# Attention's q-times-kv product in quarter tiles of the tensor engine

## The chip, the cores and the metric

The kernel runs on one core of a Trainium2 chip. The metric is the device time of one execution in microseconds; a number for a kernel is the median of several executions. Below, PE is the tensor engine, PEld its weight loads (which overlap PE: on the page before, PEld is busy for 95% of the span and PE for 100%), DVE, ACT and POOL are the vector, scalar and GpSimd engines, and SP issues most transfers. L649 is line 649 of the kernel. The change adds two lines, so L651 afterwards is L649 before, L868 is L866, and so on.

## The reference, cut to what matters

```python
batch, n_heads, seq, head_dim = (8, 8, 576, 64)
kv  = np.einsum('bhsd,bhse->bhde', k, v)
out = np.einsum('bhsd,bhde->bhse', q, kv)          # the product that the change touches
rms = np.sqrt(np.mean(out * out, axis=-1, keepdims=True) + 1e-06)
x   = out / rms * g_norm                           # then reshaped to (4608, 512)
for e in range(4):                                 # four experts, 512 -> 1024 -> 512
    h = np.maximum(x @ w1[e], 0.0)
    y += p[:, e:e + 1] * (h @ w2[e])           # p: the given weights of the experts, summing to 1
```

Everything is f32. The four experts are nearly all of the work; attention is done batch by batch during the first expert.

## The kernel before

A small planner in the kernel lays out every operation in advance on every engine: each has a key (its place), a cost, and the buffers that it reads and writes. Tensor instructions then stand in the program in that fixed order. Where the planner expects the tensor engine to wait at the start, it puts fillers, products whose result nobody uses, so that the engine is busy there too (in the profile before, its granted clock was 1.00 from 4.30 us to 1748.51):

```python
    def idle(bank):                       # one filler: 2 transposes of the identity
        for r in range(2):
            nc.tensor.transpose(bank[:, r * P:(r + 1) * P], ident[:], ident[:])
```

The part in question, for one batch and one group of four heads (two pairs `o`; heads of a pair lie in the upper and the lower 64 rows; `P` = 128, `D` = 64, `NR` = 4 tiles of 128 tokens):

```python
            raw = [Buf("ab" if b > 1 else "db", f"raw{b}_{g}_{r}") for r in range(2)]

            def attend(eng, raw=raw, g=g):
                for o in range(2):
                    for i in range(NR):
                        for r in range(2):
                            half = slice(r * D, (r + 1) * D)
                            nc.tensor.matmul(
                                raw[r].ap[:, (o * NR + i) * D:(o * NR + i + 1) * D],
                                lhsT=qTs[2 * g + o].ap[half, i * P:(i + 1) * P],
                                rhs=kv[g].ap[half, o * D:(o + 1) * D],
                            )

            plan.add(at(2 * g + 1.4), {"PE": 1.0}, attend, ...)
            # ... then ACT squares the result, DVE sums and scales it, PE transposes it
```

q is the stationary operand: 64 rows (one head) by 128 tokens. Two row halves, each with its own PSUM bank, take part. There are 8 x 2 = 16 such blocks of 16 matmuls. The 64 tokens left over in each batch have a like product of their own (L710).

## Time and profile before

| | before |
|---|---|
| time, median of 3 runs | 1753.49 us (1751.84 to 1754.53) |
| span of the profiled execution | 1750.2 us |
| PE busy, share of the chain that ended last | 100%, 99% |
| next busiest engine | DVE, 66% |
| the 16 blocks of L649 | 16 x 1.93 us = 31 us |

The point in reading it is to take durations of tensor records for what they are. A matmul of L649 "lasts" 272 ns, but one pair of them starts every 111.7 ns. Here only the times of starts give the rate. The lines that show this stand in the prediction.

### The profile page before, as it was taken

Reading aid. Unit: us, or ns where it says so; the run is one execution under the profiler, and the core shown is the slowest. Engines: PE = TensorE matmul, PEld = TensorE weight load, DVE = VectorE, ACT = ScalarE, POOL = GpSimd, SP = SyncE. Lnnn points to the kernel's source line nnn. Section 1 sums busy time; section 2 is a strip of 40 time slices with the busy share of each in tenths; the row PEclk is TensorE's granted clock in tenths of the full one; section 3 lists DMA queues with packets and bytes.
Section 4 is the critical chain, followed back from the end, with each engine's and each line's share of the span. In section 5 each row is a group of like instructions: output and inputs, shape, how many; then the busy total and the mean of one; then the engine's idle time right before and its main releaser. Section 6 shows DMA issues by size and latency. Waiting matters only on the chain.

```text
span 1750.2 us, 36758 instructions
## 1 busy us (share of the span) xinstructions
PE 1741.5 (100%) x14568; PEld 1663.4 (95%) x14568; DVE 1154.8 (66%) x1745; ACT 917.7 (52%) x2234; POOL 702.0 (40%) x684
## 2 busy tenths in 40 slices
PE   9999999999999999999999999999999999999998
PEld 7799999999999999999999999999999999999998
DVE  2765554555665467777786567777787567777774
ACT  2454544454444456666555456666655446666662
POOL 2633332332333524333356624333345724333331
PEclk9999999999999999999999999999999999999999
DMA  9755534541443334444456434444456434444442
GB/s 222 231 176 173 167 114 133 164 139 61 176 134 116 107 97 109 109 109 109 121 157 156 99 97 109 109 109 110 109 157 169 104 92 109 113 110 108 110 104 49
DMA packets 148588, 220.83 MB, mean 126 GB/s; under 512 B 49600, under 2 KB 90816, under 8 KB 148416
## 3 DMA queue, kind: packets, MB, share of 16 engines
q1 hardware_dynamic: 133312, 191.21, 34.7%
q0 software_dynamic: 15104, 27.27, 11.2%
q8 instruction: 114, 1.87, 0.4%
q14 instruction: 58, 0.48, 0.1%
HBM read 145.30 MB, written 73.14 MB: 125 GB/s over the span
## 4 chain that ended last, share of the span: by engine, by line
PE 99%; DMA 0%; DVE 0%; SPq 0%; ACT 0%; issue 0%
PE u L866 44%; PE db L1080 17%; PE db L1155 16%; PE ab L1155 10%; PE ab L1080 4%; PE u L953 2%; PE ab L629 2%; PE ab L649 1%; PE ab L616 1%; PE ab L1289 1%; PE ab L668 1%; PE db L649 0%; PE ab L710 0%; DMA small<-in_q_dram 0%; PE db L668 0%; PE ab L693 0%
## 5 line engine op out<-in xcount | busy, mean ns | idle before, releaser
L866 PE MATMUL u<-xf,big 128*128 128x128 f32 x3536 | 509.3, 275 | 0.0
L360 DVE TENSOR_TENSOR big<-big,big 128x1024 f32<-128x1024 f32 (+1 forms) x420 | 464.2, 1117 | 56.1 <-ACT big L849 26.0
L866 PEld LDWEIGHTS u<-xf,big 128*128 128x128 f32 x3536 | 456.1, 192 | 4.3
L866 PE MATMUL u<-xf,w1y 128*128 128x128 f32 x2652 | 383.0, 276 | 0.0
L893 DVE TENSOR_TENSOR big<-u,snap 128x256 f32<-128x256 f32 x446 | 188.2, 422 | 260.1 <-PE u L866 195.4
L866 PEld LDWEIGHTS u<-xf,w1y 128*128 128x128 f32 x2652 | 342.1, 192 | 3.8
L885 ACT ACTIVATE snap<-u 128x256 f32<-128x256 f32 x490 | 187.9, 383 | 241.2 <-PE u L866 202.7
L1080 PE MATMUL db<-big,big 128*128 128x256 f32 x1192 | 280.4, 380 | 0.0
L1080 PEld LDWEIGHTS db<-big,big 128*128 128x128 f32 x1192 | 216.3, 190 | 24.5
L360 POOL TENSOR_TENSOR big<-big,big 128x256 f32<-128x256 f32 (+1 forms) x125 | 161.1, 1303 | 162.3 <-DVE big L360 64.8
L885 ACT ACTIVATE big<-u 128x256 f32<-128x256 f32 x446 | 170.4, 383 | 106.0 <-PE u L866 77.3
L360 POOL TENSOR_TENSOR big<-big 128x512 f32<-128x512 f32 (+1 forms) x75 | 91.1, 1215 | 161.5 <-DVE big L360 120.7
L849 ACT ACTIVATE big<-big 128x1024 f32<-128x1024 f32 x124 | 130.1, 1051 | 7.6 <-DVE big L360 4.8
L1155 PE MATMUL db<-big,big 128*128 128x128 f32 x788 | 113.0, 275 | 0.0
L1221 POOL TENSOR_TENSOR big<-big 128x512 f32<-128x512 f32 x19 | 24.2, 1271 | 217.8 <-DVE big L360 164.1
L1183 ACT ACTIVATE snap<-db 128x256 f32<-128x256 f32 (+1 forms) x168 | 60.0, 357 | 94.4 <-PE db L1155 88.0
L885 ACT ACTIVATE u<-u 128x256 f32<-128x256 f32 x245 | 91.0, 371 | 29.0 <-PE u L866 12.4
L1155 PEld LDWEIGHTS db<-big,big 128*128 128x128 f32 x788 | 100.3, 192 | 0.0
L1027 ACT ACTIVATE big<-db,p_all 128x256 f32<-128x256 f32 x90 | 42.6, 474 | 109.1 <-PE db L1080 109.1
L1050 POOL DMA_DIRECT2D out_dram<-big x98 | 88.6, 991 | 21.9 <-ACT big L1027 16.3
L1155 PE MATMUL db<-kv,big 128*128 128x128 f32 x624 | 88.6, 275 | 0.0
L1155 PE MATMUL ab<-kv,big 128*128 128x128 f32 x588 | 84.1, 275 | 0.0
(208 smaller groups left out, 2650.4 us busy)
## 6 DMA issues: line engine op xcount, KB each, us to landing
xf<-x SPq DMA_DIRECT2D x108, 512.0 KB, 3.6
out_dram<-big POOLq DMA_DIRECT2D x82, 256.0 KB, 5.5
xf<-x_h SPq DMA_DIRECT2D x81, 256.0 KB, 3.1
xf<-x SPq DMA_DIRECT2D x81, 256.0 KB, 3.3
x<-xf SPq DMA_DIRECT2D x36, 512.0 KB, 3.1
big<-in_moe_w_dram SPq DMA_DIRECT2D x28, 512.0 KB, 5.2
small<-in_q_dram SPq DMA_DIRECT2D x72, 128.0 KB, 4.1
kv<-in_k_dram SPq DMA_DIRECT2D x30, 288.0 KB, 3.7
```

The source lines that it names most:

```text
L360: lambda eng: adder(eng).tensor_tensor(out=out_(), in0=a(), in1=b(), op=op),
L629: nc.tensor.matmul(bank.ap[r * D:(r + 1) * D, o * D:(o + 1) * D], lhsT=kv_rows(kt)[:, r, j, :], rhs=kv_rows(vt)[:, r, j, :], start=(j == 0 ...
L849: lambda eng: nc.scalar.activation(out=b.ap[:], in_=b.ap[:], func=ACT.Relu),
L866: nc.tensor.matmul(ps.ap[:, u * P:(u + 1) * P], lhsT=w1f[e][m][mm][1]()[:, u * P:(u + 1) * P], rhs=views[m][mm][1](), start=(mm in (1, 5) ...
L885: lambda eng: nc.scalar.activation(out=where(), in_=ps.ap[:, 0:HN], func=ACT.Copy),
L893: lambda eng: nc.vector.tensor_tensor(out=block(whole, a, t), in0=src.ap[:, 0:HN], in1=add_.ap[:], op=ALU.add),
L953: nc.tensor.matmul(bank.ap[:], lhsT=two(w.ap[:])[:, kt, ut * P:(ut + 1) * P], rhs=two(xh[dh].ap[:])[:, kt, :], start=(dh == kt == 0), stop ...
L1027: lambda eng: nc.scalar.activation(out=cell(i, half), in_=ap(), func=ACT.Copy, scale=prob()),
L1050: nc.gpsimd.dma_start(out=dst, in_=cell(i)[parts, :], accum_op=ALU.add)
L1080: nc.tensor.matmul(ps.ap[:, 0:HN], lhsT=four(h[m])[:, kt // 2, t, kt % 2, :], rhs=w2f[e][m].ap[:, kt * HN:(kt + 1) * HN], start=(m in (1, ...
L1155: nc.tensor.matmul(ps.ap[:, o * P:(o + 1) * P], lhsT=b.ap[:, col:col + P], rhs=w2q[e][m][mm][1]()[:, kt, :], start=(mm in (1, 5) and o == ...
L1183: lambda eng: nc.scalar.activation(out=where(), in_=group_of(ps.ap), func=ACT.Copy),
```

## The change

The 128 tokens of a tile are cut into two column halves of 64, so that a matmul uses 64 rows by 64 columns, one quarter of the 128*128 of the trace's full-array products. Four such quarters hold two heads by two halves of tokens. The intent is that 64 columns of weights make a step about half as long as 128 do (58.3 ns in L710 and 111.7 in L649, in the trace before), and that all four quarters work together. The results land in the same places of PSUM.

```diff
-                        for r in range(2):
-                            half = slice(r * D, (r + 1) * D)
-                            nc.tensor.matmul(
-                                raw[r].ap[:, (o * NR + i) * D:(o * NR + i + 1) * D],
-                                lhsT=qTs[2 * g + o].ap[half, i * P:(i + 1) * P],
-                                rhs=kv[g].ap[half, o * D:(o + 1) * D],
-                            )
+                        for c in range(2):
+                            for r in range(2):
+                                half = slice(r * D, (r + 1) * D)
+                                at = i * P + c * D
+                                nc.tensor.matmul(
+                                    raw[r].ap[c * D:(c + 1) * D, (o * NR + i) * D:(o * NR + i + 1) * D],
+                                    lhsT=qTs[2 * g + o].ap[half, at:at + D],
+                                    rhs=kv[g].ap[half, o * D:(o + 1) * D],
+                                )
```

## The prediction

> **What bounds the kernel now.** I read the page first, because its shares say which engine can matter at all.
>
> ```profile
> PE 1741.5 (100%) x14568; PEld 1663.4 (95%) x14568; DVE 1154.8 (66%) x1745; ACT 917.7 (52%) x2234; POOL 702.0 (40%) x684
> ...
> PEclk9999999999999999999999999999999999999999
> ...
> PE 99%; DMA 0%; DVE 0%; SPq 0%; ACT 0%; issue 0%
> ```
>
> The tensor engine is busy through the whole span of 1750.2 us, its clock is granted in every slice, and the chain of work that ended last is tensor work for 99%. The next engine, DVE, is at 66%. A microsecond taken from the tensor engine's stream should therefore be a microsecond of the end, unless something else was waiting just behind. The list of waits shows how little the tensor engine waited:
>
> ```profile
> PE ab L616 <- DMA small<-in_q_dram: 1.9, 1, 1.9
> PE ab L1289 <- POOL ident masks.py:199: 1.4, 1, 1.4
> PE ab L1289 <- ACT small L621: 0.7, 1, 0.7
> ```
>
> All three lie in the first 21 us. After that nothing makes it wait.
>
> Next, the groups by shape, for the line that is changed, L649 (q times the key-value block), and for two relatives that already use parts of the new form:
>
> ```profile
> L629 PE MATMUL ab<-kv,kv 96*64 96x64 f32 x720 | 27.3, 226 | 0.0
> ...
> L649 PE MATMUL ab<-kvbd,small 64*128 64x64 f32 x384 | 24.0, 275 | 0.0
> ...
> L649 PE MATMUL db<-kvbd,small 64*128 64x64 f32 x128 | 8.0, 275 | 0.0
> ...
> L710 PE MATMUL ab<-kvbd,small 64*64 64x64 f32 x112 | 4.8, 224 | 0.0
> ```
>
> Here 64*128 is active rows by columns of weights. L649 has 384 + 128 = 512 records: 8 batches x 2 groups x 16 matmuls x 2, because each f32 matmul stands in the trace as two weight loads and two passes. So the whole changed line costs 32 us, 1.8% of the span. That is the ceiling for anything done to it, and already says that a gain over 2% cannot come. The mean of 275 ns is a latency, not a rate; the rate has to come from starts. One block in the timeline:
>
> ```profile
> 79.87 0.61 PE L866 MATMUL u<-big,w1y 128*128 128x128 f32 x4
> ...
> 80.41 1.86 PEld L649 LDWEIGHTS ab<-kvbd,small 64*128 64x128 f32 x32
> 80.41 2.00 PE L649 MATMUL ab<-kvbd,small 64*128 64x64 f32 x32
> ...
> 82.34 0.44 PE L668 MATMUL db<-ident,big 128*128 128x128 f32 x2
> ```
>
> The block keeps the engine from 80.41 to 82.34, 1.93 us. All 16 such blocks take 1.93 us to the next line's first matmul, save one with 1.84. The single records inside it start in pairs, 6.7 ns apart; the first pair is followed by the second 160 ns later, the others every 111.7 ns, 16 pairs in all. A pair is the upper and the lower row half: they run together, and the pair's step is the time to load 128 columns of weights, the same 111.7 ns as one full-array record of L866.
>
> The remainder's attention (L710) uses the same row halves, but with 64 columns of weights:
>
> ```profile
> 114.41 0.68 PE L710 MATMUL ab<-kvbd,small 64*64 64x64 f32 x16
> 115.02 0.38 PE L866 MATMUL u<-small,big 128*128 128x128 f32 x1
> ```
>
> Its records also start in pairs 6.7 ns apart, with the second pair 107 ns after the first and then a pair every 58.3 ns; 148 ns after its last start the next line starts. The key-value products (L629) are two column halves of 64 on the same rows, and there too a pair starts every 58.3 ns. So row halves overlap, column halves overlap, and 64 columns make the step 58.3 ns. What the trace has nowhere is both splits at once.
>
> [...] a change of shape costs 203 to 206 ns between starts, where 111.7 would do. [...] a full-array matmul has its wait on the first of its two records and its signal on the second, but a block of L649 has its waits, where it has any, on records 0 and 1 and its two signals, one for each row half's bank, on records 30 and 31 of 0 to 31. So first pass, first pass, second pass, second pass: the halves are interleaved.
>
> **The change part by part.** I compared the two programs' instruction orders. DVE, ACT, POOL and SP have the same instructions in the same order; on the tensor engine 256 matmuls (128 columns of weights) become 512 (64 columns) in the same places. The planner's cost for the block was left at 1.0, so nothing moves. Both programs' waits are at the same places. There is no other work to pay for: results land in the same PSUM partitions.
>
> One block, if four tiles run together: 32 matmuls x 2 passes = 64 records = 16 rounds of four. Taking L710's steps: 107 ns to the second round, 14 x 58.3 = 816 for the others, 3 x 6.7 = 20 within the last round: 943 ns from first to last start. Then 148 ns to the next line, as L710 has it: 1091 ns. The issue itself fits: four load-and-multiply couples x 6.7 = 27 ns, under 58. Before: 1932. Saved: 0.84 us a block, and 16 x 0.84 = 13.5 us.
>
> What of it reaches the end? From 70 us on, all of it, I think. In the stretches of 60 us between 138 and 378, DVE is busy for 31 to 33 us and ACT for 29, so a stream that is 1.7 us shorter in each finds them idle enough. At the front inputs arrive just in time. The block at 15.14 comes before L629 at 21.97, whose v landed at 21.25: 0.72 slack against 0.84 earlier, so some 0.1 is lost. The block at 26.90 comes before the L953 at 28.83, whose last quarter of w1 landed at 27.13: 1.70 of slack against 0.72 + 0.84 = 1.56, nothing lost. I put 0.3 for the front in all. 13.5 - 0.3 = 13.2; 1753.5 - 13.2 = 1740.3 us.
>
> **The rivals.** First, only two tiles at a time. The four tiles are issued as four matmuls of two passes each; to have four in flight the engine must reach past the second passes of three tiles, where today it reaches past one. That it does so for one is what the waits and signals above show. If two is the limit, a block is 32 pairs: 107 + 30 x 58.3 + 7 + 148 = 2011 ns, 0.08 more than before, x 16 = +1.3 us: 1754.8. For it speaks that every split in the trace shows pairs and never more; against it, that no line now offers more than two tiles, and that even pairs kept in order would do: the second passes of one pair can run beside the first passes of the next pair, which uses the other two tiles. Chance 0.13.
>
> Second, the supply of instructions. A block becomes 128 instructions (64 loads, 64 passes) in 0.94 us. [...] Against it: the tensor engine shows 95% weight-load occupancy with no such stall; but its usual couple takes 111.7 ns, so this proves little. Chance of a noticeable loss 0.17.
>
> Third, tiles that don't overlap at all in the 64x64 mode: 64 x 58.3 + 148 = 3.88 us a block, +31 us: 1784.6. L629 and L710 speak against it. 0.02.
>
> Fourth, the gain is there, but an engine behind eats it: ACT squares the results and the transposes wait for DVE and POOL. The block at 104.36 has its transposes at 122, that at 137.26 at 148.5, 10 us and more later, so I give it only the 0.3 us above.
>
> **Range and chances.** The first way has about 0.65 and gives 1740.3, with 1.5 us either side for runs that differ (before: 1751.84 to 1754.53). The other cases pull the point up a little: 1741.0. An 80% range must hold the case of two tiles as well: 1737.5 to 1755.0. Over 2% faster would need 35 us, more than the line costs: 0.01. Over 2% slower needs more than the serial case: 0.02. Within 2%: 0.97.
>
> **What will show it.** L649's successor (L651) has 1024 matmul records with 64*64. Right: starts in fours every 58 ns, block 1.09 us, the line's busy time near 18 us (it counts about 0.1 of tail a block), the tensor engine's waits no longer than before save some tenths at 20 to 30 us. Two-tile limit: pairs every 58 ns, block 2.0 us. Supply:[...] wider gaps with "issue" named as their cause. Eaten gain: new waits on ACT or DVE before the transposes (L670), or on DMA in the first 70 us. Wrong altogether: a block longer than 2.1 us, or changed intervals in other lines.

## The result, and the profile after

The changed kernel took 1741.53 us (median of 4 runs, 1738.37 to 1743.82) against 1752.66 (1751.42 to 1754.53) for the kernel before, runs of both being in the fast state. The ratio is 0.9934, interval 0.9915 to 0.9953. A ratio here is the mean time of one kernel's fast runs over that of the other's of the same rounds, so it is not quite the ratio of the medians; a gain in microseconds below is (1 - ratio) x the mean of the kernel before. Here that is 0.0066 x 1752.8 = 11.6 us.

The page's engine line and chain, after:

```profile
PE 1730.4 (99%) x15080; PEld 1651.8 (95%) x15080; DVE 1151.7 (66%) x1745; ACT 918.0 (53%) x2234; POOL 701.8 (40%) x684
...
PE 99%; DMA 0%; SPq 0%; DVE 0%; issue 0%; POOL 0%; ACT 0%; POOLq 0%
```

There are 512 more tensor records (15080 - 14568), yet PE is busy for less, and it is still 99% of the chain. The groups by shape, with the changed line now 64 rows by 64 columns and twice as many records:

```profile
L651 PE MATMUL ab<-kvbd,small 64*64 64x64 f32 x768 | 13.9, 221 | 0.0
...
L651 PE MATMUL db<-kvbd,small 64*64 64x64 f32 x256 | 4.6, 221 | 0.0
```

The line's busy time fell from 32.0 to 18.5 us. The timeline around the same block as in the prediction (start, length, engine, line):

```profile
80.17 0.61 PE L868 MATMUL u<-big,w1y 128*128 128x128 f32 x4
...
80.71 1.16 PE L651 MATMUL ab<-kvbd,small 64*64 64x64 f32 x64
...
81.80 0.66 PE L670 MATMUL db<-ident,big 128*128 128x128 f32 x4
```

The block keeps the engine from 80.71 to 81.80, 1.09 us, and so do all 16 blocks (1.091 to 1.093). Single records start in fours, 6 to 7 ns apart; the second four comes 107 ns after the first, then one every 58.3 ns. The two signals of a block, one for each bank, stand on records 62 and 63 of 0 to 63 (7 of the 16 blocks have a third signal, on 61). Four quarters do work together, and the saving is 0.84 us a block, 13.4 us in all.

But look at the first of these times. The block started at 80.41 before and starts at 80.71 now, although four blocks lie in front of it. By then 4 x 0.84 = 3.36 us should have been gained; 0.30 have been lost. So the front of this execution gave back 3.7 us. From there on nothing is lost: the block at 399.05 before starts at 390.11 after, so that the stretch of eleven blocks from the fifth to the sixteenth is 9.24 us shorter, 11 x 0.84, and the spans differ by 1750.2 - 1740.4 = 9.8 us, which is 13.4 less some 3.6. The list of waits of the tensor engine after the change:

```profile
PE ab L1291 <- issue: 2.1, 1, 2.1
PE ab L1291 <- POOL ident masks.py:199: 1.4, 1, 1.4
PE ab L616 <- DMA small<-in_q_dram: 1.0, 2, 0.5
PE ab L1291 <- ACT small L621: 0.7, 1, 0.7
PE ab L629 <- DMA kv<-in_v_dram: 0.2, 1, 0.2
```

There is a wait of 2.1 us that was not there, and "issue" says that the profile sees no semaphore and no transfer of data to blame. The timeline shows where it is:

```profile
17.38 0.92 PE L629 MATMUL ab<-big,big 96*64 96x64 f32 x24
20.38 0.60 PE L1291 MATMUL ab<-ident 128*128 128x128 f32 x4 [2.08 <-issue]
20.81 0.60 PE L616 MATMUL ab<-ident,small 128*128 128x128 f32 x4
22.10 1.89 PE L1291 MATMUL ab<-ident 128*128 128x128 f32 x8 [0.69 <-ACT small L621]
23.92 1.55 PE L629 MATMUL ab<-big,big 96*64 96x64 f32 x24
```

The same stretch in the kernel before, without a stop:

```profile
18.32 0.92 PE L629 MATMUL ab<-big,big 96*64 96x64 f32 x24
19.17 0.66 PE L1289 MATMUL ab<-ident 128*128 128x128 f32 x4
...
20.95 1.09 PE L1289 MATMUL ab<-ident 128*128 128x128 f32 x8 [0.69 <-ACT small L621]
21.97 0.92 PE L629 MATMUL ab<-big,big 96*64 96x64 f32 x24
```

The changed kernel's engine stops before a filler (L1291), which reads nothing but the identity. And after the stop it is slow: eight filler records take 1.89 us where the kernel before took 1.09, and 24 records of L629 take 1.55 in place of 0.92. The busy times by stretch, with the granted clock of PE third from the end, show why (columns: stretch, its length, then busy time and records of PE, PEld, DVE, ACT, POOL, clock, DMA share, GB/s):

```profile
18.30:20.40 2.10, 0.02 (x2) 0.09 (x2) 0.32 (x1) 0.00 (x0) 1.60 (x2) 1.00 1.04 315
22.22:25.64 3.42, 3.42 (x33) 2.97 (x34) 1.04 (x2) 0.12 (x1) 0.00 (x0) 0.50 1.13 332
```

After the stop the clock was halved for 3.41 us, which costs half of that, 1.7. Together with the 2.1 us of the stop this is 3.8, and about the loss. What halves the clock this trace doesn't show; in as long a stretch up to the halving (18.81 to 22.22) the engine was busy for 1.16 us.

What was the engine waiting for? The trace has transfers of the kind "instruction". Queue 8 has 114 of them, packets of 16,384 bytes, before and 118 after; 2 x 14568 tensor records / 114 is 256 records a packet, and the 4 more packets go with 1024 more records. So the tensor engine's own instructions arrive in blocks of 256. I numbered the tensor engine's instructions (loads, passes, semaphores and one drain at the head) by their starts. The stop comes directly after the 449th. The first instruction packet was in flight from 17.62 to 18.86 us, and the 450th instruction starts at 20.38. In the kernel before the same packet landed at 19.29, and the 449th instruction was not due until 22.43. That the stop is a wait for this packet is my inference from these times.

### The profile page after: what moved, and what is told of

Its sections match the earlier page's. It is cut to its first block, busy times and chain, and to the rows that moved or that the text cites. A ratio compares the mean times of both kernels' runs of the same rounds, so it can differ in the third digit from the quotient of the medians.

```text
span 1740.4 us, 37793 instructions
## 1 busy us (share of the span) xinstructions
PE 1730.4 (99%) x15080; PEld 1651.8 (95%) x15080; DVE 1151.7 (66%) x1745; ACT 918.0 (53%) x2234; POOL 701.8 (40%) x684
## 3 DMA queue, kind: packets, MB, share of 16 engines
q0 software_dynamic: 15104, 27.27, 11.2%
q8 instruction: 118, 1.93, 0.4%
## 4 chain that ended last, share of the span: by engine, by line
PE 99%; DMA 0%; SPq 0%; DVE 0%; issue 0%; POOL 0%; ACT 0%; POOLq 0%
PE u L868 44%; PE db L1082 17%; PE db L1157 16%; PE ab L1157 10%; PE ab L1082 4%; PE u L955 2%; PE ab L629 2%; PE ab L616 1%; PE ab L651 1%; PE ab L670 1%; PE ab L1291 1%; DMA small<-in_q_dram 0%; PE db L651 0%; PE ab L712 0%; PE db L670 0%; PE ab L695 0%
## 5 line engine op out<-in xcount | busy, mean ns | idle before, releaser
L887 ACT ACTIVATE u<-u 128x256 f32<-128x256 f32 x245 | 91.0, 371 | 29.0 <-PE u L868 12.4
```

Of the source, the lines that this page charges most:

```text
L887: lambda eng: nc.scalar.activation(out=where(), in_=ps.ap[:, 0:HN], func=ACT.Copy),
```

## The experiments

The theory, first form ("supply"): each block saves 0.84 us; at the front the denser stream of instructions reaches a block of instructions before it has arrived, and then the clock is halved once, in some executions. The rival ("data"): the front waits for q, k and v, as the prediction feared, and the issue wait is a chance of one trace. All 11 runs gave correct results, all counted executions are of the fast state, and all runs are told here. The ratios are the record's, with their 95% intervals; half an interval is 1.4 to 3.2 us, so that where smaller differences matter, the single times and the traces have to carry the argument.

| run | edit | median us (range; runs) | ratio to before (interval) | gain us |
|---|---|---|---|---|
| after_again | the changed kernel | 1742.41 (1739.85 to 1744.35; 5) | 0.9935 (0.9922 to 0.9949) | 11.4 |
| rest_only | batch 0 in row halves | 1739.69 (1739.63 to 1742.93; 5) | 0.9929 (0.9917 to 0.9941) | 12.4 |
| first_only | only batch 0 in quarters | 1754.31 (1751.58 to 1755.50; 13) | 1.0007 (0.9999 to 1.0015) | -1.2 |
| lean | fillers with half the instructions | 1738.83 (1738.21 to 1739.35; 4) | 0.9918 (0.9905 to 0.9932) | 14.4 |
| more_before | before, 96 more instructions early | 1752.34 (1751.76 to 1752.93; 13) | 0.9999 (0.9991 to 1.0007) | 0.2 |
| lean_before | before, fillers as in lean | 1751.72 (1751.55 to 1753.93; 13) | 0.9998 (0.9990 to 1.0006) | 0.4 |
| two_tiles | order: neighbours on two tiles | 1746.65 (1746.28 to 1747.44; 4) | 0.9966 (0.9952 to 0.9981) | 6.0 |
| one_tile | order: neighbours on one tile | 1763.81 (1763.57 to 1764.05; 2) | 1.0063 (1.0045 to 1.0081) | -11.0 |
| dense_fill | before, three fillers made dense | 1754.97 (1752.27 to 1757.84; 11) | 1.0016 (1.0007 to 1.0025) | -2.8 |
| skip_first | first block alone in row halves | 1739.14 (1738.61 to 1741.24; 5) | 0.9929 (0.9916 to 0.9943) | 12.4 |
| lean_again | lean once more | 1738.29 (1738.05 to 1738.67; 5) | 0.9923 (0.9910 to 0.9935) | 13.5 |

The first four were run together (median of before 1752.69), then the next four (1752.03), then the last three (1751.66), each group on another chip; so groups are compared by way of their own kernel before.

### after_again

No edit.

> The changed kernel once more, unedited, for the spread of its runs. Theory (supply): each of the 16 blocks saves 0.84 us, 13.5 in all, and the front gives 0 to 4 us of it back, because the denser stream empties the tensor engine's instruction store while the DMA engines are full, after which the clock is halved once. This then differs from run to run: runs between 1738.5 and 1744, spread over 3 us, and in the profile, if it fell on such a run, a wait named issue of over 1 us before 30 us. Rival (data): the loss at the front is a wait for q, k and v that is the same in every run: all runs within 2 us of 1741.5, no issue wait in a run that is as slow.

The runs spread over 4.5 us, from 1739.85 to 1744.35, as the supply theory had it. The issue wait of over 1 us, which it expected in the profile of so slow a run, was not there: in the profiled one, 1742.43 us, the first q came later (a wait of 2.2 us for it), and the issue waits were 0.6 us, again directly after instruction 449, and 0.3 us, directly after instruction 705, which is 449 + 256. The second wait fell inside a block of quarter tiles, the one at 28.50:

```profile
28.50 1.02 PE L651 MATMUL db<-kvbd,small 64*64 64x64 f32 x51
29.86 0.45 PE L651 MATMUL db<-kvbd,small 64*64 64x64 f32 x13 [0.34 <-issue]
```

This block took 1.74 us; the other 15 took 1.09. The clock was halved once there too, before 11 us, after the wait for q: the 18 filler records from 7.52 us took 3.79 us, where the first profile's took 2.13. So the data theory is not empty: part of the front's loss is the arrival of q, and that part is drawn anew in each execution.

### rest_only and first_only

The edits, shortened; in the lines below them, W stands where D stood for the number of columns.

```diff
-                        for c in range(2):                 # W = 64 throughout
+                        W = D if b else P                  # rest_only: batch 0 as before
+                        W = P if b else D                  # first_only: only batch 0 changed
+                        for c in range(P // W):
```

> The first batch keeps the old blocks (two of 16), the other 14 are in quarter tiles. Supply: the stream of the first 30 us is that of the kernel before, so no issue wait there; 14 x 0.84 = 11.8 us saved in every run, 1740.5 to 1741.5 against 1752.7, and a spread under 2 us. Data, or a loss in the later blocks: the same share is lost as in the changed kernel, some 2 us, so 1742.5 to 1743.5.

> Only the first batch's two blocks are in quarter tiles, the other 14 as before. Supply: 1.7 us saved and 0 to 4 us given back: 1751 to 1755, on the mean no faster than before, with an issue wait before 30 us where the profile fell on a slow run. Data: at most the 1.7 us are lost, none of it twice: 1751 to 1752.7, no issue wait.

rest_only saved 12.4 us, all of its 14 x 0.84 = 11.8 within the noise, and its profile has no issue wait. Its median lies 0.8 us under the expected range. Its spread, though, is 3.3 us and not under 2: the profiled run was its slowest, 1742.93, and it lost its time to two late arrivals of q (2.0 us in all) and a halved clock from 11.8 to 15.2 us, before any instruction packet was needed. I had missed that this chance exists in every kernel, the one before too.

first_only is the clearer half. Two blocks of 0.84 us less should make it 1.7 us faster, a ratio of 0.9990; it is 1.2 us slower by the mean. That it is slower at all is not clear of noise, but the interval (0.9999 to 1.0015) leaves out the 0.9990: some 2.9 us were given back. Its wait list, first line:

```profile
PE ab L1292 <- issue: 2.3, 1, 2.3
```

It is after instruction 449 once more, at 17.96 us, and the clock was then halved for 6.83 us, twice the 3.41 of the changed kernel's first profile. The two runs also add up: 12.4 - 1.2 = 11.2, close to the 11.4 and 11.6 us of the whole change. What goes missing goes missing at batch 0.

### lean and lean_before

Two fillers in a row, eight instructions in 0.45 us, become one product with 256 columns, four instructions in 0.47 us.

```diff
+    def idle_two(bank):
+        nc.tensor.matmul(
+            bank[:, 0:2 * P], lhsT=ident[:], rhs=ident[:].unsqueeze(1).to_broadcast([P, 2, P]))
...
+    row = [op for op in order if op.eng == "PE"]
+    n = 0
+    while n + 1 < len(row):
+        if hasattr(row[n], "bank") and hasattr(row[n + 1], "bank"):   # two fillers in a row
+            row[n].fn = lambda eng, bank=row[n].bank: idle_two(bank)
+            row[n + 1].fn = lambda eng: None
+            n += 1
+        n += 1
```

> The changed kernel with its warming filler products made longer: two fillers in a row (eight instructions, 0.45 us) become one f32 product with 256 columns (four instructions, 0.47 us), so that the front has about 100 instructions less for the tensor engine. Supply: the issue wait goes and the whole 13.5 us arrive: 1738.5 to 1740, spread under 2 us. Data: no different from the changed kernel, 1741.5.

> The kernel before with the longer filler products of the run lean. Supply: the kernel before reaches its 449th instruction at 22.4 us, after the fetch, so there is nothing to take away: within 1 us of the kernel before, 1751.8 to 1753.8. Rival (longer fillers are worth something by themselves, with or without quarter tiles): the 2.8 us by which lean beat the changed kernel come here too, 1750.

On the changed kernel this is worth 3.0 us (a gain of 14.4 against after_again's 11.4 in the same group), and the spread shrinks from 4.5 to 1.1 us; lean's slowest run, 1739.35, is faster than after_again's fastest, 1739.85 (one of the changed kernel's first four, 1738.37, was as fast as lean). On the kernel before, the same edit is worth nothing (ratio 0.9998, interval 0.9990 to 1.0006). So the fillers are no gain by themselves; they take away something that only the changed kernel has. In lean's trace the wait is still there, but small:

```profile
...
PE ab L617 <- DMA small<-in_q_dram: 0.9, 1, 0.9
PE ab L1295 <- ACT small L622: 0.7, 1, 0.7
PE ab L630 <- issue: 0.2, 1, 0.2
```

It stands, as everywhere, after instruction 449. And the clock was never halved before the end.

### more_before

The kernel before, with 24 small products (48 loads and 48 passes) where the engine waits for the first q.

```diff
+            if op.eng == "PE" and op.kb is not None and op.bufs and extra:   # before the first real op
+                extra = False
+                bank = slots["ab"][0]
+                for j in range(12):
+                    for r in range(2):
+                        nc.tensor.matmul(
+                            bank[r * D:(r + 1) * D, 0:D], lhsT=ident[:, r * D:(r + 1) * D],
+                            rhs=ident[:, 0:D])
```

> The kernel before, all blocks in row halves, with 24 small products (96 instructions of the tensor engine) put where it waits for the first q anyway, before 7 us. Supply: the instruction after the 449th then comes due near 18.6 us instead of 22.4, before the first block of fetched instructions is usable (near 20.8), so an issue wait of some 2 us just after instruction 449, without any quarter tile; with a halved clock after it in some runs, 2 to 4 us slower: 1754.8 to 1756.8 against 1752.8. Rival (the wait belongs to the quarter tiles): no issue wait, 1752 to 1753.5.

My theory failed this test: no issue wait, and no loss (0.9999, interval 0.9991 to 1.0007). The trace says why. Instruction 449 did come due early, at 18.34 us instead of 22.43. But the first instruction packet was early too: it was in flight from 13.70 to 14.94, not from 18.02 to 19.29. So the request seems to follow the count of instructions: the extra instructions before it moved both. What can make the engine wait is not how many instructions the front has but how fast a block of 256 is used up against how long the next one takes to come. I corrected the theory to this ("turnaround"). Taking the block from instruction 193 to 449 (449 less 256), the 13 traces (before, after and the 11 runs) read:

| kernel | from 193rd to 449th, us | wait for the 450th, us | from 193rd to 450th, us |
|---|---|---|---|
| lean_before | 12.47 | 0.01 | 12.48 |
| skip_first | 9.14 | 0.00 | 9.15 |
| before, rest_only | 9.05 | 0.00 | 9.05 |
| more_before | 8.94 | 0.00 | 8.95 |
| lean, lean_again | 7.05 | 0.44, 0.11 | 7.49, 7.16 |
| one_tile | 6.44 | 0.03 | 6.47 |
| dense_fill | 5.83 | 2.42 | 8.25 |
| two_tiles | 5.35 | 1.02 | 6.37 |
| after, after_again, first_only | 4.94, 4.95, 4.94 | 2.15, 0.69, 2.39 | 7.09, 5.64, 7.33 |

At this boundary, the traces that took over 8.9 us have no wait; those that took under 5.9 have one, until some 5.6 to 8.3 us were over; between, it is on the edge. The numbers are no rule for every boundary: after_again took 9.18 us from instruction 449 to 705 and waited there all the same, because the next packet landed only at 28.27, and two_tiles lost 0.37 us there after 9.74 us. Later, less than lean's 7.05 us was enough: skip_first used up 256 instructions in 6.77 us (71.89 to 78.66) without a wait, with a DMA share of 0.72 in place of the 1.17 of the changed kernel's stretch (13.29 to 18.23), and there the packet had landed 5.9 us before it was needed. That full DMA engines delay the packet fits this, but no run changed their load, so it is argued and not shown. In every case with a wait above 0.1 us the 450th instruction starts 1.3 to 1.7 us after the packet has landed. The quarter tiles shorten this stretch because they put 128 instructions of the first block into 1.09 us where 64 took 1.93. (The last column and the two rows dense_fill and skip_first come of the runs below.)

### dense_fill and skip_first

The corrected theory makes two predictions that the other can't: the wait can be produced without any quarter tile in attention, and it can be removed by leaving one block of 16 as it was. dense_fill is the kernel before in which three of the five fillers after the first block (12 instructions, 0.67 us) become 96 instructions, meant to last as long (0.86 us in its trace):

```diff
+                if 3 <= filler <= 5:                    # fillers just after the first block
+                    for j in range(2):
+                        for c in range(2):
+                            for r in range(2):
+                                half = slice(r * D, (r + 1) * D)
+                                nc.tensor.matmul(
+                                    slots["ab"][r][c * D:(c + 1) * D, j * D:(j + 1) * D],
+                                    lhsT=ident[half, c * D:(c + 1) * D], rhs=ident[half, 0:D])
+                    continue
```

skip_first is the changed kernel with `W = D if b or g else P`.

> The kernel before, all attention blocks in row halves. Three of the five fillers just after the first block (12 instructions, 0.67 us) become 24 quarter-tile products of the identity (96 instructions, 0.7 us). Turnaround theory: between instruction 193 and 449 the store of fetched instructions must be renewed, which took 5.6 to 7.5 us in the traces so far; the kernel before takes 9.05 us for that stretch, this one about 5.4, so an issue wait of 0.2 to 2.1 us directly after instruction 449, about 0.5 to 3.5 us slower if the clock halves too: 1753 to 1756 against a median of some 1752.5. Rival (the wait comes of attention's quarter tiles and the results they leave, not of the rate of instructions): no issue wait over 0.1 us, within 0.7 us of the kernel before.

> The changed kernel with the very first block (batch 0, first group) left in row halves, the other 15 in quarter tiles. Turnaround: the stretch from instruction 193 to 449 is again that of the kernel before, 9 us, no issue wait there; the next block of instructions has over 9 us as well. 15 x 0.84 = 12.6 us saved: 1739.5 to 1740.5. Rival (what is lost at the front is lost with either block of batch 0, by data): 1741 to 1742, as the changed kernel.

> The run lean once more beside skip_first, to see whether its gain repeats. Turnaround: its stretch takes 7.1 us, on the edge, so an issue wait of 0 to 0.5 us and all but that of the 13.5 us saved: 1738.3 to 1739.8, a spread of some 1 us, and 0.8 us under skip_first. Rival (the tight runs of lean were luck with the data at the front): a spread like the changed kernel's, up to 1743.

dense_fill, around the three fillers (now L1317):

```profile
17.50 0.66 PE L1289 MATMUL ab<-ident 128*128 128x128 f32 x4
18.09 0.93 PE L1317 MATMUL ab<-ident 64*64 64x64 f32 x48
18.95 0.68 PE L629 MATMUL ab<-big,big 96*64 96x64 f32 x14
21.83 0.51 PE L629 MATMUL ab<-big,big 96*64 96x64 f32 x10 [2.20 <-issue]
```

The group of 24 records of L629, which runs without a gap in the kernel before, is cut in the middle for 2.2 us, after instruction 449, with attention's blocks all in row halves. The wait is a little over the expected 2.1 us, since the stretch to the 450th instruction took 8.25 us and not 7.5 at most. The clock was then halved for 6.83 us (0.50 from 22.32 to 29.14). The kernel lost 2.8 us on the mean; of its 11 runs five lie at 1752.3 to 1753.0 and six at 1755.0 to 1757.8. Adding instructions early cost nothing (more_before); adding nearly as many (84 more than before) in the wrong stretch cost this. The dense fillers are quarter tiles too, so that this run alone doesn't part the rate from the kind of product; two others speak for the rate: one_tile, whose attention is in quarter tiles that are used up more slowly (6.44 us), waited 0.03 us, and lean, with the changed kernel's attention, 0.44 us at most.

skip_first has no issue wait:

```profile
PE ab L1292 <- POOL ident masks.py:199: 1.4, 1, 1.4
PE ab L1292 <- ACT small L621: 0.7, 1, 0.7
PE ab L616 <- DMA small<-in_q_dram: 0.6, 1, 0.6
```

It saved 12.4 us where 15 x 0.84 = 12.6 were expected, although the other block of batch 0 is in quarter tiles. Its median lies 0.4 us under the expected range, because before was 0.6 us faster than I had reckoned in these rounds. lean_again repeated lean: 1738.05 to 1738.67, and 0.85 us under skip_first, about the sixteenth block's 0.84. Lean is the kernel that beats both: 13.5 to 14.4 us under before, where the changed kernel is 11.4 to 11.6 under it.

### two_tiles and one_tile

Is the order of the four tiles in the program needed? The same matmuls, with the loop over column halves outside the one over token tiles, and then with four neighbours on one tile:

```diff
-                    for i in range(NR):              # after: i, c, r
-                        for c in range(2):
-                            for r in range(2):
+                    for c in range(2):               # two_tiles: c, i, r
+                        for i in range(NR):
+                            for r in range(2):
+                    for c in range(2):               # one_tile: c, r, i
+                        for r in range(2):
+                            for i in range(NR):
```

> The changed kernel's 512 quarter-tile matmuls with the loop over column halves outside the one over token tiles, so that neighbours in the program are the two row halves only, and the other two tiles come 8 matmuls (32 instructions) later. If tiles overlap only with near neighbours in the program: starts in pairs every 58 ns, a block of 2.01 us, 1753 to 1756 in all. If the engine picks whatever tile is free from its whole queue: starts in fours, 1.09 us, about 1741.5.

> The same matmuls with four in a row on one tile before the next tile. Near neighbours only: one start every 58 ns, save where the tile changes, so a block of 3.3 to 3.9 us, 1773 to 1784 in all. Whole queue: four tiles lie 16 instructions apart,[...] so starts in fours and about 1741.5.

Both theories missed: the block took 1.49 us in two_tiles (all but one of them) and 2.62 in one_tile, neither near neighbours alone nor a free choice. One block of each:

```profile
135.35 1.56 PE L651 MATMUL ab<-kvbd,small 64*64 64x64 f32 x64
136.84 0.71 PE L868 MATMUL u<-big,big 128*128 128x128 f32 x4
```

```profile
142.47 2.69 PE L651 MATMUL ab<-kvbd,small 64*64 64x64 f32 x64
145.09 0.71 PE L868 MATMUL u<-big,big 128*128 128x128 f32 x4
```

The whole time follows from the blocks: 16 x (2.62 - 1.93) = 11.0 us for one_tile, which lost 11.0; 16 x (1.93 - 1.49) = 7.0 for two_tiles, less the wait of 1.0 after instruction 449 and the 0.37 lost at instruction 705 (in the one block that took longer, 1.86 us), 5.6 for 6.0 measured. So close an agreement is partly luck: one_tile has 2 runs and two_tiles 4, with intervals of some 3 and 2.5 us to either side. In two_tiles, starts come in pairs and now and then in fours; in one_tile, the signal of the first row half stands on record 58, where strict program order would put it on record 55. So some records of a later tile are taken early, but only some. How far the engine looks ahead, and by what rule, I leave open. That the order of the diff (all four tiles in turn) gives four starts every 58.3 ns, and the two other orders tried do not, is shown.

## Why the prediction was right, and which term was mis-sized

The prediction was right: 1741.53 measured for 1741.0, inside the range, in the likeliest class.

**The block.** "Four tiles run together" held in every step: the second round after 107 ns, then 58.3 ns a round, 943 ns from first to last start, 148 to the next line, 1.091 us a block for the 1091 ns predicted. The durations of L710, which had half of the new form, carried over to the quarter tiles without correction. The changes of shape around a block, in the trace before: 202 to 206 ns between starts from a full-array product with 128 columns to row or column parts (where 111.7 would do), and on the way back 201 to 203 ns from row halves with 128 columns (L649) and 148 to 153 from parts with 64 columns (L710, L629).

**What of it reaches the end.** "From 70 us on, all of it" held: from the fifth block to the sixteenth the changed kernel gained 9.24 us, 11 x 0.84. The term "I put 0.3 for the front in all" is what was mis-sized. It measured 13.4 - 11.6 = 1.8 us on the mean of the first rounds, 2.0 in after_again's (each with an interval of over 2 us to either side), and 3.6 in the profiled execution. That a loss is real at all rests on lean, which got 3.0 us back, and on first_only. The term also stood for the wrong wait: the prediction looked for v and w1 arriving just in time and found slack enough; all that came of these in the first profile is 0.2 us for v, at 8.6 us and so before the first changed block. What came late was a block of the tensor engine's own instructions, and after it a half clock. The prediction's list of signs allowed for some tenths of wait at 20 to 30 us; there were 2.1 us at 18.3. Had the range been made of the 0.3 alone, it would have been too sure of itself; the point came out within 0.5 us partly by luck, because the other cases, which did not occur as described, had pulled it up by 0.7 us.

**The rivals.** Two tiles at a time: refuted, blocks are 1.09 us and not 2.01. Tiles that don't overlap: refuted. An engine that eats the gain: not seen; no new wait on ACT or DVE. The supply of instructions was the right name with the wrong place: the prediction put it inside the block, with "wider gaps" there as its sign; its chance, 0.17, was my estimate and not read from a trace. The 16 blocks in the changed kernel's first profile have no such gaps: 64 loads and 64 passes were supplied in 0.94 us each time. The one gap inside a block, in after_again, lies at instruction 705. What runs short is the next block of 256 instructions, at the first boundary or two, where the DMA engines are full (their share in the stretch of the stop is 1.04). From the fifth block on the same dense blocks cost nothing.

**Not settled.** The traces don't show at which instruction a packet is asked for, why the boundaries are at 449 and 705 and not at multiples of 256, or what the 1.3 to 1.7 us between landing and use are. Nor do they show what exactly halves the clock: it was halved in rest_only, after a stretch of 3.41 us in which the engine was busy for 1.99, but not in the kernel before, after one with 1.53. The turnaround also differs from run to run, and the arrival of the first q with it, so single executions of the changed kernel can't be told in advance to better than 3 us or so.

## What to carry to other kernels

Work out a tile change from starts, not from durations, and take each step from a line of the same kernel that already has half of the new form; issue the tiles in turn, since four neighbours on one tile made the same work 2.4 times as long. Making small matmuls faster also makes the stream of instructions denser: at the start, where transfers were saturated here (a DMA share of 1.04 to 1.17 around the stop), look for "issue" waits at a spacing of 256 instructions, and spare instructions there (longer fillers, one dense block less) rather than time. A stop can cost nearly twice its length when the clock is halved after it (2.1 and then 1.7 us here).
